# Second layer of the first mixture turned round: weights stationary, shares multiplied into h, output kept by columns

## The chip, the cores and the metric

The kernel runs on one core of a Trainium2 chip. Its time is the device time of one execution in microseconds (us); lower is better. Engines are named as in the profile: PE is TensorE (matmuls; PEld its weight loads), DVE VectorE, ACT ScalarE, POOL GpSimd, SP the queue that issues nearly all DMAs.

## What is computed

Three stages, all in float32. First an attention with random features (4 batches, 8 heads, 576 tokens, head width 64) gives `x`, 2304 tokens by 512. Then two mixtures of experts:

```python
# first mixture: 4 experts, every token through every expert, weighted by its share p
p = domain_probs / (domain_probs.sum(-1, keepdims=True) + 1e-09)
out = np.zeros((N, D), dtype=np.float32)          # N = 2304, D = 512, F = 1024
for e in range(E):
    h = np.maximum(x @ w1[e], 0.0)
    out += p[:, e:e + 1] * (h @ w2[e])
...
# second mixture: 32 slots, 8 experts of 4 slots each; x is now the output of the first
logits = x @ phi
d = softmax of logits over the tokens             # axis 0
slot_input = d.T @ x
for e in range(E):
    h = np.maximum(slot_input[e] @ w1[e], 0.0)
    slot_out[e] = h @ w2[e]
c = softmax of logits over the slots              # axis 1
out = c @ slot_out
```

## The kernel before

Nearly all of the time is the first mixture. Its two layers are cut into 24 **units**: 8 groups of weights (4 experts, each hidden width of 1024 in two groups of 512; `G`) times 3 blocks of 768 tokens (`b`), block innermost. In a unit each layer is one 2x2 block product done with seven products instead of eight (Winograd's form of Strassen's rule; I1 to I7, issued as I1, I2, I6, I5, I7, I3, I4). The first three units compute their first layer plainly, with eight products (`plain1`). Every float32 operand is split into a rounded part (`...h`) and the rest (`...l`), both in the fp32r format, and a product is the sum of three matmul passes, high-high, high-low and low-high.

A first-layer product (`pass1`, line 586) holds 128x128 of w1 stationary and streams 384 token columns of x: 12 matmuls. It leaves h transposed, hidden width on the partitions, tokens along the columns. A second-layer product (`product2`, line 793) holds 128 tokens of h stationary and streams 256 columns of w2: 3 token tiles x 2 x 3 passes = 18 matmuls. Its result has tokens on the partitions, so that the token's share `pr` is one number per partition, and `to_x2` (line 775) adds `pr` times the result to the output tile `x2`, three instructions of 256 columns for each quarter of the output.

PE's order is written out by hand in `pieces`: the first-layer product of unit u and the second-layer product of unit u-1 take turns. What DVE and ACT do between them (sums of the seven products, relu, splitting h into high and low parts) is queued by `evacuate1` and `rest` with a delay in products (`after(d, ...)`, counted down by `tick`). The first-layer results use two PSUM accumulators, X and B, of two banks each and one buffer each; the second layer has two more, so that all eight banks are in use. An accumulator is written again only when all its readers are done. The splitting of the input blocks into the operands of the seven products (`whole`, `block_sum`, `block_split`) runs on DVE and ACT in units 0 to 4, at places given by a table (`prep_steps`).

The second mixture needs, before its experts, a running softmax over the tokens: the **slot work**. For a block of tokens it turns x2 (`slot_turn`, tile tpm), forms logits (`slot_logits`, lq; `slot_sum`, lt), takes the running maximum on DVE and the exponentials on ACT, turns them back (`slot_back`, dp) and gathers `d.T @ x` (`slot_gather`, acc). In the kernel before there are five such blocks (512 tokens, the last 256). So that it can start early, the last two units run their second layer in two parts, two token tiles and then one (`SPLIT`, `LO`, `HI_`; tiles Xq, Bq), with two PSUM banks instead of four, and slot tasks are popped from a list between products.

Behind that comes a tail: 32 tiles of 1 MB of the second mixture's weights (`w2t`), three of them loaded early (`pre`), the others as the memory of the first mixture comes free, in the order of a list (`order`); `hidden` (line 1241), `second_layer` (line 1269) and the output (`out_pair`, line 1295).

## Time and profile before

| | |
|---|---|
| Time, median of 3 runs | 970.72 us (969.58 to 973.63) |
| Profiled execution | 970.0 us, of which 968.2 us lie between the first and the last instruction (the span) |
| PE busy | 944.9 us, 98% of the span |
| DVE, ACT, POOL busy | 699.6, 502.1, 348.2 us (72%, 52%, 36%) |
| DMA | 227.18 MB, 235 GB/s over the span |
| Granted TensorE clock | 0.998 of full speed |

Busy times come from instruction records of that one execution. Matmuls overlap in the pipeline: a record of one lasts 0.28 to 0.34 us, while the next starts 0.12 to 0.17 us later, so a busy PE is not PE at its best, and the time of a product is read from one start to the next. The waits of an engine are put down to what ended them.

### The profile page before, as it was taken

To read this page: it belongs to the slowest core of one execution; us is meant where nothing else is said; L and a number is where in the kernel's file an instruction comes from. 1 tells how busy PE (TensorE), PEld (TensorE's weight loads), DVE (VectorE), ACT (ScalarE), POOL (GpSimd) and SP (SyncE) were. 2 spreads that over 40 slices of the span, in tenths; PEclk is the share of its full clock that TensorE was granted. 3 is DMA by queue.
4 is the path that set the end of the run, shared out by engine and by line. 5 is a ranking of instruction groups with operands and counts; after the bars stand their busy time and mean duration, and the time that the engine had idled before them with its cause. 6 is when DMAs were issued, how large, how long until landed. Compare 5 with 4: busy or idle time off the path is not lost.

```text
span 968.2 us, 18074 instructions
## 1 busy us (share of the span) xinstructions
PE 944.9 (98%) x7070; PEld 902.8 (93%) x7070; DVE 699.6 (72%) x1268; ACT 502.1 (52%) x940; POOL 348.2 (36%) x288
## 2 busy tenths in 40 slices
PE   8999999999999999999999999999999999998997
PEld 8999989999999999999999999999999999796644
DVE  7888885998788766678667687666786667757432
ACT  5899885544554443555444545435454444435322
POOL 7878882343414340443234143404432341000000
PEclk9999999999999999999999999999999999999999
DMA  8688776756787757676666566565656564438997
GB/s 283 187 253 285 246 227 242 224 189 234 268 275 258 232 183 252 226 262 221 234 196 220 188 236 224 185 231 196 224 184 235 193 218 158 133 126 342 380 419 316
DMA packets 63220, 227.18 MB, mean 235 GB/s; under 512 B 8352, under 2 KB 17696, under 8 KB 59040
## 3 DMA queue, kind: packets, MB, share of 16 engines
q1 hardware_dynamic: 59392, 215.81, 65.3%
q10 hardware_dynamic: 3744, 10.23, 2.7%
q8 instruction: 56, 0.92, 0.4%
q14 instruction: 28, 0.23, 0.1%
HBM read 202.42 MB, written 23.59 MB: 233 GB/s over the span
## 4 chain that ended last, share of the span: by engine, by line
PE 88%; DVE 7%; ACT 3%; issue 1%; DMA 1%; SPq 0%; ACTq 0%; DVEq 0%
PE X L586 20%; PE X L793 18%; PE B L586 15%; PE B L793 13%; PE kv L220 3%; PE num L244 3%; PE Xq L793 2%; PE pj L176 2%; PE so L1269 2%; PE Bq L793 1%; PE pj L177 1%; PE pj L178 1%; PE hq L1241 1%; PE tp L234 1%; PE tpx L265 1%
## 5 line engine op out<-in xcount | busy, mean ns | idle before, releaser
L417 POOL TENSOR_TENSOR Tw<-raww 128x512 f32<-128x512 f32 x30 | 43.3, 1465 | 200.1 <-DMA raww<-wl 200.1
L586 PE MATMUL B<-x,w1h 128*128 128x384 f32 x432 | 110.3, 336 | 0.7 <-PE X L793 0.7
L586 PE MATMUL X<-x,w1h 128*128 128x384 f32 x432 | 110.4, 336 | 0.1
L586 PE MATMUL X<-x,w1x 128*128 128x384 f32 x504 | 94.8, 336 | 0.1
L653 DVE TENSOR_TENSOR u<-B,u 128x768 f32<-128x768 f32 x23 | 22.0, 957 | 99.5 <-PE B L586 99.5
L201 ACT ACTIVATE fe<-pj,nb 128x128 f32<-128x128 f32 x288 | 83.2, 390 | 10.0 <-DVE nb L194 9.2
L586 PEld LDWEIGHTS X<-x,w1x 128*128 128x128 f32 x504 | 86.0, 188 | 2.2 <-issue 1.9
L586 PEld LDWEIGHTS B<-x,w1h 128*128 128x128 f32 x432 | 75.4, 189 | 0.9 <-PE X L793 0.9
L586 PEld LDWEIGHTS X<-x,w1h 128*128 128x128 f32 x432 | 75.5, 189 | 0.2 <-PE Xq L793 0.2
L586 PE MATMUL X<-x,w1l 128*128 128x384 f32 x216 | 72.3, 335 | 0.0
L586 PE MATMUL B<-x,w1l 128*128 128x384 f32 x216 | 72.3, 335 | 0.0
L436 POOL TENSOR_TENSOR w2l<-Tw,w2h 128x512 fp32r<-128x512 f32 x32 | 43.3, 1354 | 43.3 <-ACT w2h L435 43.3
L436 POOL TENSOR_TENSOR w2l<-raww,w2h 128x512 fp32r<-128x512 f32 x24 | 31.8, 1325 | 74.6 <-ACT w2h L435 74.5
L184 DVE TENSOR_REDUCE stat<-pj 128x4 f32<-128x512 f32 x72 | 49.5, 687 | 10.0 <-PE pj L178 9.1
L151 POOL TENSOR_TENSOR lo<-raw,hi 128x512 fp32r<-128x512 f32 x35 | 44.8, 1279 | 20.0 <-ACT hi L148 19.4
L436 POOL TENSOR_TENSOR w1l<-raww,w1h 128x512 fp32r<-128x512 f32 x25 | 38.7, 1550 | 34.5 <-ACT w1h L435 34.5
L635 ACT CAST s3h<-X 128x768 fp32r<-128x768 f32 x21 | 16.9, 804 | 65.8 <-DVE X L573 61.9
L436 POOL TENSOR_TENSOR w1x<-Tw,w1x 128x512 fp32r<-128x512 f32 x21 | 29.1, 1386 | 52.4 <-ACT w1x L435 52.4
L586 PE MATMUL B<-x,w1x 128*128 128x384 f32 x252 | 47.4, 336 | 0.0
L176 PE MATMUL pj<-om_hi,hi 128*128 128x256 f32 x144 | 45.1, 313 | 1.6 <-ACT fe L201 1.1
L775 DVE SCALAR_TENSOR_TENSOR x<-B,pr,x 128x256 f32<-128x256 f32 x108 | 45.6, 478 | 1.3
L840 ACT COPY v<-X 128x768 f32<-128x768 f32 x42 | 33.7, 802 | 18.1 <-PE X L793 17.6
(306 smaller groups left out, 3209.5 us busy)
## 6 DMA issues: line engine op xcount, KB each, us to landing
x<-xt SPq DMA_DIRECT2D x84, 768.0 KB, 4.4
x<-xd SPq DMA_DIRECT2D x75, 768.0 KB, 4.5
raww<-wl SPq DMA_DIRECT2D x16, 1024.0 KB, 7.6
w2tb<-w2l SPq DMA_DIRECT2D x11, 1024.0 KB, 10.3
raw<-ql SPq DMA_DIRECT2D x18, 512.0 KB, 4.4
xd<-xst SPq DMA_DIRECT2D x36, 256.0 KB, 2.8
raw<-kl SPq DMA_DIRECT2D x16, 512.0 KB, 4.6
w2ta<-w2l SPq DMA_DIRECT2D x5, 1024.0 KB, 9.4
```

The source lines that it names most:

```text
L151: (nc.gpsimd if i else nc.vector).tensor_tensor(out=lo, in0=r, in1=f32(hi), op=ALU.subtract)
L176: nc.tensor.matmul(o, lhsT=hi[:, pi, :], rhs=om_hi, start=True, stop=False)
L184: nc.vector.tensor_reduce(out=stats(i)[:, 4 * g:4 * g + 4, 0], in_=pjs[i, g], axis=AX.X, op=ALU.max)
L201: nc.scalar.activation(out=feats[i][:, 4 * g + h, :], in_=pjs[i, g][:, h, :], func=AF.Exp, bias=biases[i, g][:, h:h + 1], scale=1.0,)
L220: nc.tensor.matmul(kvps[b][h // 4][:, h % 4, :], lhsT=feats[i][p0:p0 + np_, h, :], rhs=v[p0:p0 + np_, h, :], start=first and h % 4 == 0, s ...
L244: nc.tensor.matmul(num[p0:p0 + n, h, :], lhsT=fts[i][:, 4 * g + h, p0:p0 + n], rhs=kvt[b][:, 4 * g + h, :], start=True, stop=True,)
L417: nc.gpsimd.tensor_tensor(out=out_, in0=a, in1=b_, op=op)
L436: nc.gpsimd.tensor_tensor(out=lo, in0=src, in1=f32(hi), op=ALU.subtract)
L586: nc.tensor.matmul(o, lhsT=lhs[:, jp, c], rhs=rhs[:, :, k, :], start=first and not k and not n, stop=False, skip_group_check=True,)
L775: nc.vector.scalar_tensor_tensor(out=o, in0=src, scalar=w, in1=o, op0=ALU.mult, op1=ALU.add)
L793: nc.tensor.matmul(q[:, n, :], lhsT=lhs[:, jp, p, :], rhs=rhs[:, jp, :], start=i in (I1, I2, I7) and n % 2 == 0 and jp == 0 and m == 0, st ...
L840: nc.scalar.copy(out=v("v1"), in_=q)
```

## The change

- **Second layer turned.** `product2` now holds 128x128 of w2 stationary and streams 384 token columns of h: 2 column tiles x 2 x 3 passes = 12 matmuls. The result has output columns on the partitions; `x2` is kept so ([P, 4, 768] for each token block).
- **Shares into h.** A share now varies along the columns. The shares are turned once, kept in DRAM (`prd`), and for each unit one DMA spreads 768 of them over all partitions (`load_share`, tile prb). `scaled` replaces the relu: max(q, 0) times the share, on DVE, once for each of the four quarters of h. Since h carries the share, the second-layer result is added to `x2` with one instruction for each of the seven products (`evacuate2`); in the first group ACT copies four of them instead.
- **No split ending.** The last two units run like the others. All slot work stands behind the last first-layer product, between the seven second-layer products of the last unit (`ENDING`), in six blocks of 384 tokens. Logits are formed straight from x2; x2 is still turned for the gather.
- **Around it.** The table of `prep_steps` has other places, memory is laid out anew, five weight tiles instead of three are loaded early, and the shares of the second mixture (`slot_shares`) are computed at once behind the slot work. Token halves are now tiles 0-2 and 3-5.

```diff
-        for n, p in enumerate(ps):
-            for jp in range(2):
-                for m, (lhs, rhs) in enumerate(((h, wh), (h, wl_), (l, wh))):
-                    nc.tensor.matmul(
-                        q[:, n, :], lhsT=lhs[:, jp, p, :], rhs=rhs[:, jp, :],
+        for c in range(2):
+            cs = slice(c * P, (c + 1) * P)
+            for jp in range(2):
+                for m, (lhs, rhs) in enumerate(((wh, h), (wl_, h), (wh, l))):
+                    nc.tensor.matmul(
+                        q[:, c, :], lhsT=lhs[:, jp, cs], rhs=rhs[:, jp, :],
...
+    def evacuate2(u, i, q):
+        G, b = units[u]
+        half, n = {I1: (0, 0), I2: (0, 0), I6: (1, 0), I4: (1, 0), I5: (1, 1), I7: (1, 1), I3: (0, 1)}[i]
+        o = x2[b][:, 2 * n:2 * n + 2, half * TH:(half + 1) * TH]
+        if G or i in (I2, I4, I7):
+            nc.vector.tensor_tensor(out=o, in0=q, in1=o, op=ALU.add)
         else:
-            nc.vector.scalar_tensor_tensor(out=o, in0=src, scalar=w, in1=o, op0=ALU.mult, op1=ALU.add)
+            nc.scalar.copy(out=o, in_=q)
...
+    def load_share(u):
...
+        nc.sync.dma_start(
+            out=t.rearrange("p a (n t) -> p (a n) t", n=NP),
+            in_=prd[TB * b:TB * b + TB, GROUPS[G][0], :].partition_broadcast(P),
+        )
+
+    def scaled(u, out, in0, half):
+        w = prb[u][:, half, :].unsqueeze(1).to_broadcast([P, 2, TH])
+        nc.vector.scalar_tensor_tensor(out=out, in0=in0, scalar=0.0, in1=w, op0=ALU.max, op1=ALU.mult)
...
         elif i == I7:
...
+            r = pair(tmp("r22"))
+            if not plain:
+                tt(r, q, pair(L["u4"]), ALU.add)
+            scaled(u, r, q if plain else r, 1)
+            done.add(("r22", u))
         elif i == I3:
...
-            plus(s1, q, pair(L["u4"]), ALU.add)
-            plus(q, q, r11, ALU.subtract)
...
+            scaled(u, o, q, 1)
+            q = o
+            tt(s1, q, pair(L["r22"]), ALU.add)
+            tt(q, q, r11, ALU.subtract)
+            after(0, ("s2", u), lambda: tt(s2, s1, r11, ALU.subtract))
...
-    SPLIT = "q1 P1 q2 q6 P2 q5 P6 q7 q3 P5 q4 r1 P7 r2 r6 P3 r5 P4 r7 r3 r4"
-    ENDING = "q1 t t q2 t q6 t q5 t q7 t q3 t q4 t t r1 r2 r6 t r5 r7 t r3 t r4"
...
+    ENDING = (
+        "l0 P1 l1 t0 P2 t1 l2 b0 P6 a0 t2 l3 b1 P5 a1 t3 g0 P3 b2 a2 l4 g1 P7 b3 a3 t4 g2 P4 b4 a4 g3"
+    )
...
-            (2, 8): [(W, 2, KH[2])],
-            (2, 10): [(W, 2, KH[3])],
+            (2, 9): [(W, 2, KH[2])],
+            (2, 10): [(S, 1, I7)],
```

In `ENDING`, P1 to P4 are the products of the last unit and l, t, a, b, g the five slot steps (logits, sum, turns, back, gather) with the number of the token block.

How the order of instructions changes, at three places (PE's and DVE's rows without their numbers; "x2" at a row's end is a count).

PE, in the middle of the program: the end of one first-layer product into B and the beginning of the second-layer product that follows it; before, the triple of L793 stands six times.

```order
L586 MATMUL B_5629<-x,w1h 128x384 x2
L586 MATMUL B_5629<-x,w1l 128x384
L793 MATMUL B_5652<-w2h,e12h 128x256
L793 MATMUL B_5652<-w2l,e12h 128x256
L793 MATMUL B_5652<-w2h,e12l 128x256
```

Of the change, the same place in the last units (the triple of L771 stands four times):

```order
L597 MATMUL B_9079<-x,w1h 128x384 x2
L597 MATMUL B_9079<-x,w1l 128x384
L771 MATMUL B_9095<-e22h,w2h 128x384
L771 MATMUL B_9095<-e22h,w2l 128x384
L771 MATMUL B_9095<-e22l,w2h 128x384
```

The second layer's rows are as wide as the first layer's now, and there are 12 of them where there were 18.

DVE in unit 21 (token block 2, so that x_2 is written by unit 20's second layer), from first-layer product I7 to I4. Before:

```order
L653 TENSOR_TENSOR u_9539<-B_9571,u_9539 128x768
L836 TENSOR_TENSOR v_9565<-B_9592,v_9565 128x768
L775 SCALAR_TENSOR_TENSOR x_2_3673<-v_9565,pr,x_2_3673 128x256 x3
L573 SCALAR_TENSOR_TENSOR s_9627<-X_9397,u_9539 128x768
L573 SCALAR_TENSOR_TENSOR X_9397<-X_9397,u_9410 128x2x384
L699 TENSOR_TENSOR s_9628<-s_9627,u_9410 128x768
L639 TENSOR_TENSOR s3l<-X_9397,s3h 128x768
L775 SCALAR_TENSOR_TENSOR x_2_3673<-X_9418,pr,x_2_3673 128x256 x3
L653 TENSOR_TENSOR B_9571<-B_9571,u_9499 128x2x384
L573 SCALAR_TENSOR_TENSOR e12l<-B_9571,e12h 128x768
L573 SCALAR_TENSOR_TENSOR u_9499<-B_9571,s_9628 128x768
```

Of the change:

```order
L654 TENSOR_TENSOR r_8576<-B_8563,u_8534 128x768
L584 SCALAR_TENSOR_TENSOR r_8576<-r_8576,prb 128x768
L793 TENSOR_TENSOR x_2_3573<-B_8585,x_2_3573 128x2x384
L584 SCALAR_TENSOR_TENSOR X_8413<-X_8413,prb 128x2x384
L654 TENSOR_TENSOR s_8611<-X_8413,r_8576 128x768
L654 TENSOR_TENSOR X_8413<-X_8413,u_8426 128x2x384
L654 TENSOR_TENSOR s_8612<-s_8611,u_8426 128x768
L648 TENSOR_TENSOR s3l<-X_8413,s3h 128x768
L793 TENSOR_TENSOR x_2_3573<-X_8432,x_2_3573 128x2x384
L654 TENSOR_TENSOR B_8563<-B_8563,u_8497 128x2x384
L584 SCALAR_TENSOR_TENSOR s_8659<-B_8563,prb 128x768
L648 TENSOR_TENSOR e12l<-s_8659,e12h 128x768
```

Three multiplications by the share (L584) have come in here, one of them ahead of the four instructions that read the accumulator X, and each group of one addition and three L775 has become one addition (L793).

PE at the end of the slot work, just ahead of the first `hidden` matmul. Before, from the last turns behind the last product of the last unit on:

```order
L1013 MATMUL tpm<-ident,x_2_3673 128x128 x6
L1074 MATMUL dp<-ident,mo 128x64 x4
L1013 MATMUL tpm<-ident,x_2_3673 128x128 x2
L1092 MATMUL acc<-x_2_3673,d 32x512 x4
L1022 MATMUL lq<-x2t,phis 32x256 x4
L78 MATMUL warm<-om_hi 128x256 x2
L1033 MATMUL lt<-mo,sumr 128x256
L78 MATMUL warm<-om_hi 128x256 x7
L1074 MATMUL dp<-ident,mo 128x32 x2
L1174 MATMUL tps<-sf,mo 128x32 x4
L1182 MATMUL acc<-x_2_3673,d 32x512 x2
L1174 MATMUL tps<-sumr,mo 128x32 x4
```

Of the change, from the last product on:

```order
L996 MATMUL dp<-ident,mo 128x64 x3
L932 MATMUL tpm<-ident,x_2_3573 128x128 x12
L1014 MATMUL acc<-sp_u_9334,keep 32x512
L1014 MATMUL acc<-sp_s_9341,keep 32x512
L1014 MATMUL acc<-sp_s_9348,keep 32x512
L945 MATMUL lq<-x_2_3573,phis 32x384 x4
L932 MATMUL tpm<-ident,x_2_3573 128x128 x8
L955 MATMUL lt<-mo,sumr 128x384
L1014 MATMUL acc<-mo,keep 32x512 x2
L1014 MATMUL acc<-sp_u_9292,keep 32x512
L932 MATMUL tpm<-ident,x_2_3573 128x128 x4
L996 MATMUL dp<-ident,sp_u_9245 128x32 x3
```

The chain of the last block is the same in kind; the turns of the last two blocks, which stood partly ahead of the last products, and one gather more stand behind them now.

## Rows read from the trace of the kernel before

**Rows 1.** The page: engines, and one DMA issue (count, KB each, us to landing).

```profile
PE 944.9 (98%) x7070; PEld 902.8 (93%) x7070; DVE 699.6 (72%) x1268; ACT 502.1 (52%) x940; POOL 348.2 (36%) x288
...
x<-xt SPq DMA_DIRECT2D x84, 768.0 KB, 4.4
```

**Rows 2.** Busy time by stretch: PE, PEld, DVE, ACT, POOL, granted clock, DMA share, GB/s.

```profile
480.00:520.00 40.00, 40.00 (x286) 40.00 (x286) 31.93 (x43) 20.92 (x30) 16.12 (x12) 1.00 0.65 215
```

**Rows 3.** The chain that ended last: start, us until the next piece, engine, line.

```profile
174.89 2.08 PE X L586 x12
...
760.83 2.08 PE B L586 x12
762.91 2.15 PE B L793 x18
...
918.05 7.07 PE hq L1241 x64
```

**Rows 4.** The same chain, slot work on PE near the end.

```profile
861.23 0.87 PE tpm L1013 x8
...
886.51 1.07 PE lq L1022 x8
...
889.21 0.86 PE lt L1033 x2
...
895.31 1.07 PE acc L1092 x8
...
914.09 1.08 PE tps L1174 x8
```

**Rows 5.** The same chain, one slot sum on DVE and ACT.

```profile
873.25 0.61 DVE mt L1041
874.08 0.79 ACT mo L1045 x2
874.89 0.59 ACT mo L1048
```

**Rows 6.** PE in order of time, two waits of the slot work, the last product.

```profile
875.52 0.46 PE L1074 MATMUL dp<-ident,mo 64*128 64x64 f32 x4 [1.42 <-ACT mo L1048]
...
907.26 0.28 PE L793 MATMUL Bq<-w2h,e22l 128*128 128x256 f32 x1
```

**Rows 7.** DVE in order of time, instructions of units in mid program.

```profile
503.40 0.96 DVE L639 TENSOR_TENSOR s3l<-X,s3h 128x768 fp32r<-128x768 f32 x1
...
530.67 0.94 DVE L573 SCALAR_TENSOR_TENSOR s<-X,u 128x768 f32<-128x768 f32 x1
531.54 0.95 DVE L573 SCALAR_TENSOR_TENSOR X<-X,u 128x768 f32<-128x768 f32 x1
...
540.03 1.27 DVE L775 SCALAR_TENSOR_TENSOR x<-B,pr,x 128x256 f32<-128x256 f32 x3
...
571.34 2.05 DVE L639 TENSOR_TENSOR s1l<-s,s1h 128x768 fp32r<-128x768 f32 x1
```

**Rows 8.** PE in order of time, the next unit's first product into X.

```profile
506.66 0.52 PE L586 MATMUL X<-x,w1h 128*128 128x384 f32 x2
```

**Rows 9.** Waits of the whole run: us in total, times, longest.

```profile
DVE u L653 <- PE B L586: 99.5, 22, 6.2
...
DVE v L836 <- PE B L793: 22.5, 19, 1.2
```

**Rows 10.** DMA issues by SP in order of time, and the last weight tile's landing.

```profile
870.48 4.46 SPq L1228 DMA_DIRECT2D w2ta<-w2l  x5
...
901.82 7.55 SPq L1228 DMA_DIRECT2D w2tb<-w2l  x9
...
933.02 0.33 SPq L1228 DMA_DIRECT2D w2t__10926<-w2l  x1
...
w2t__10926<-w2l SPq DMA_DIRECT2D x1, 1024.0 KB, 19.8
```

**Rows 11.** PE in order of time, the matmuls that read that tile.

```profile
955.53 1.05 PE L1269 MATMUL so<-w2t__10926,ht 128*32 128x256 f32 x16
```

More of the change, by code (lines that the diff above doesn't have):

```diff
@@ L693, in evacuate1 @@
+            r = pair(L["u1"])
+            o = r if plain else q
+            scaled(u, o, q, 0)
+            high(0, I1, o)
+            if not plain:
+                after(3, ("r11", u), lambda: nc.scalar.copy(out=r, in_=q))
+            low(0, I1, o)
+        elif i == I7:
+            r = pair(tmp("r22"))
+            if not plain:
+                tt(r, q, pair(L["u4"]), ALU.add)
+            scaled(u, r, q if plain else r, 1)
+            done.add(("r22", u))
         elif i == I3:
             s1, s2, r11 = pair(tmp("s1")), pair(tmp("s2")), pair(L["u1"])
-            plus(s1, q, pair(L["u4"]), ALU.add)
@@ L883, in body @@
     pieces = []
-    for u in range(NU - 2):
+    for u in range(NU):
         for i in range(8 if u < XB else 7):
+            if u + 1 < NU and i == 0:
+                pieces.append(lambda u=u: load_share(u + 1))
             pieces.append((plain if u < XB else up)(u, i))
@@ L989, in body @@
+    keep = lgs = None
     tot = mp.tile([P, 1], F32, name="tot")
     mrun = [mp.tile([P, 1], F32, name=f"mrun{i}") for i in range(2)]
-    def slot_tasks(b):
-        turns = [lambda i=i: slot_turn(b, i) for i in range(4)]
-        logits, total, back, gather = (lambda f=f: f(b) for f in (slot_logits, slot_sum, slot_back, slot_gather))
-        share1, share2 = (lambda f=f: f(b) for f in (slot_share1, slot_share2))
-        if b < NB - 3:
-            wait = [[]] if b == 0 else []
-            tasks = [turns[0:2], turns[2:], [], [logits], [total], [], [back], *wait, [gather], [share1], [share2]]
-        elif b == NB - 3:
-            tasks = [turns[0:2], turns[2:], [logits], [total], [], [back], [gather]]
-        else:
-            tasks = [turns[0:2], turns[2:], [logits], [total]]
-        return [lambda fs=fs: [f() for f in fs] for fs in tasks]
@@ L1007, in slot_turn, with slot_task @@
-    def slot_turn(b, i, k0=0, k1=NK):
-        if i == 0 and k0 == 0:
-            st["x2t", b] = stg.tile([P, NK, 4, P], F32, name="x2t", tag="raw")
-        tp = bank("s", "tpm").rearrange("p (k t) -> p k t", k=NK)
-        for k in range(k0, k1):
-            nc.tensor.transpose(tp[:, k, :], x2t(SB[b][0] + i)[:, k * P:(k + 1) * P], ident)
-        nc.scalar.copy(out=st["x2t", b][:, k0:k1, i, :], in_=tp[:, k0:k1, :])
+    def slot_task(s):
+        {"l": slot_logits, "t": slot_sum, "a": slot_turns, "b": slot_back, "g": slot_gather}[s[0]](int(s[1]))
@@ new lines, in body, with spare_place, slot_turn @@
+    places = {}
+    def spare_place(n):
+        if n not in places:
+            if n < 6:
+                t = w1e.tile([P, 6, DM], F32, name="mo", tag="w1x")
+                places.update({k: t[:, k] for k in range(6)})
+            else:
+                tag = ("u1", "u2", "s1", "s2", "u4", "r22")[n - 6]
+                places[n] = lt.tile([P, DM], F32, name=f"sp_{tag}", tag=tag)
+        return places[n]
+    mo = spare_place
+    def slot_turn(n, i):
+        b, c0 = n // 2, (n % 2) * TH + i * P
+        x = spare_place(4 + (n % 2) * 3 + i)
+        tp = bank("s", "tpm").rearrange("p (k t) -> p k t", k=NK)
+        for k in range(NK):
+            nc.tensor.transpose(tp[:, k, :], x2[b][:, k, c0:c0 + P], ident)
+        copy = nc.vector.tensor_copy if n == NB - 1 and i == 1 else nc.scalar.copy
+        copy(out=x, in_=tp.rearrange("p k t -> p (k t)"))
+        st["x2t", n, i] = x
@@ L1153, in body @@
     assert not later, [n for _, _, n, _ in later]
-    while side:
-        task()
+    pp["2"].release()
+    pp["T"] = bank_pool("psT", "left", (4, 5, 6, 7))
+    groups.update({"aq": [4], "bq": [5], "a": [2, 3, 0], "b": [1, 4], "c": [5, 6], "d": [7]})
     n = NB - 1
+    s2 = mo(11)
+    nc.gpsimd.memset(s2[NS * NP:P], 0.0)
+    slot_logits(n)
     slot_turn(n, 0)
-    slot_turn(n, 1, 2, 4)
-    slot_back(n - 1)
-    slot_turn(n, 1, 0, 2)
-    acc = slot_gather1(n - 1)
-    slot_logits(n)
-    slot_gather2(n - 1, acc)
-    keep_warm(2, "qx")
+    slot_turn(n, 1)
     slot_sum(n)
-    keep_warm(7, "qx")
+    slot_gather(n - 1)
+    slot_turn(n, 2)
     sf = mp.tile([P, NS], F32, name="sf")
@@ L1179, in body @@
     slots_turn(0, mo(0), sf)
-    acc = bank("aq", "acc")[0:64, :]
-    for i in range(2):
-        nc.tensor.matmul(
-            acc[32 * i:32 * i + 32, :], lhsT=st["d", n][:, i, :], rhs=x2t(NT - 2 + i), start=True, stop=True
-        )
-    s2 = mo(1)[0:64, :]
-    nc.scalar.copy(out=s2[:, 0:HD], in_=acc[:, 0:HD])
-    nc.vector.tensor_copy(out=s2[:, HD:DM], in_=acc[:, HD:DM])
-    slots_turn(1, s2, sumr[0:64, 0, :])
+    acc = slot_gather1(n)
+    nc.scalar.copy(out=s2[0:NS * NP, 0:HD], in_=acc[:, 0:HD])
+    nc.vector.tensor_copy(out=s2[0:NS * NP, HD:DM], in_=acc[:, HD:DM])
+    slots_turn(1, s2, sumr[:, 0, :])
     st["rest"]()
@@ L1352, in body @@
     wqa.release()
-    gap.release()
     prep.release()
+    stg.release()
     const.release()
```

461 lines of the change are left out of this document (179 added, 282 removed).

## The prediction

> **What bounds the kernel now.** The page first: PE is busy 98% of the span, DVE 72% [rows 1]. The stretches of 40 us come next: in the middle of the program PE is busy all the time at full clock, and DVE 31.9 of 40 us [rows 2]. So there PE alone sets the pace, and what the other engines do matters only where they make PE wait. The chain of waits says the same and gives the prices: from 174.89, where unit 1 begins, it is a train of products, 2.08 us for 12 matmuls of 384 columns and 2.15 us for 18 of 256 [rows 3]. The train, with the slot work in it, ends at 918.05, where `hidden` begins [rows 3].
>
> Between 174.89 and 918.05 lie 743.2 us. They hold 163 first-layer products (two units of 8, 21 of 7, and not unit 0's 8) and 168 second-layer products: 163 x 2.08 + 168 x 2.15 = 700.2 us. The split into two and one token tiles in the last units leaves the number of matmuls as it is. Slot work on PE, at the chain's prices [rows 4]: 72 turns in runs of 8 at 0.87 make 7.8 us, four and a half logits at 1.07 make 4.8, as many sums at 0.86 make 3.9, as many gathers at 1.07 some 5.0, two tps at 1.08 make 2.2, and turning back with the warm-up matmuls some 3.1: 26.8 us. What is left, 743.2 - 700.2 - 26.8 = 16.2 us, are waits of PE. All but about 2 us of them fall into the last two units and the slot work: the 629.5 us from 174.89 to the first product of unit 22 hold 149 and 147 products and a part of one more, 627.4 us.
>
> Behind 918.05 come 50.2 us of tail. In it PE runs without a gap worth naming to the last weights: they are asked for at 933.02, land 19.8 us later at 952.8 [rows 10], and PE reads them at 955.53 [rows 11]. So the tail is PE's work in a row with the weights' stream 3 us ahead of it.
>
> **The change part by part, from the profiled execution's 970.0 us.**
>
> *Wide second-layer products.* 168 times, 18 matmuls of 256 columns become 12 of 384: the same 4608 columns, fewer starts. The first layer's rows are this very form, at 2.08 against 2.15 us [rows 3]. Gain 0.07 x 168 = 11.8 us. The bounds: nothing, if a matmul with h streaming is no faster for its columns than now; 11.8, the whole difference.
>
> Per matmul the rows give 119 ns for 256 columns and 173 ns for 384, so a fixed part near 13 ns each at 2.4 GHz, which is the level that the granted clock of 1.00 means [rows 2, 3]. The Trainium skill, "TensorE: Matmul & The Clock Gate", section "Back-to-back issue gap", gives a fixed part of 2.5 ns for a lone stream; by that six matmuls fewer would save 15 ns a product and 2.5 us in all, and the sum below would come out 9.3 us higher. The rows are of this kernel's own pairs of weight load and matmul, so I go by them; the other is a rival below.
>
> *DVE's work.* In the first layer four multiplications by the share take the place of relus on ACT and of sums with a relu in them: four instructions more in each unit, each like the ones of 768 columns from PSUM that follow each other by 0.87 us [rows 7], so +3.5 us. In the second layer three additions of about 0.96 and four groups of three at 1.27 [rows 7], 8.0 us, become seven additions, 6.7 us. That is +2.2 us a unit. DVE now stands idle 99.5/22 = 4.5 us a unit ahead of one addition and 22.5/19 = 1.2 us ahead of another [rows 9], of some 29.6 us. So it stays under PE, with 3 us or more to spare. In the first group, where ACT copies four results, DVE has less to do than now. The early units also carry the splitting of the inputs, at new places; unit 3 has 27 of DVE's instructions in 29.2 us, and I allow 1.5 us of PE's waiting there.
>
> Where the new instruction can hurt is accumulator X. Its last reader, s3l, ends at 504.36 (503.40 + 0.96), and the next unit's first product wants X at 506.66 [rows 7, 8]: 2.3 us of slack. The multiplication ahead of the four readers takes 0.87 of it. 1.4 us are left, so PE doesn't wait. All else that PE waits for (operands split with delays of up to ten products) has more than a product of slack.
>
> Of DVE's instructions, those with both inputs in SBUF vary: 0.95 us as a rule, 2.05 at 571.34 [rows 7]. The Trainium skill, "SBUF — State Buffer", section "Who interferes with whom", says that a VectorE instruction with two SBUF inputs locks against a GpSimd one that reads SBUF. That speaks against the change: it has eight such instructions a unit where there were five. At the observed extreme of 1.1 us each they would cost DVE 3.3 us more in a unit, about its spare time.
>
> *The share's DMA.* 24 times 0.39 MB, half of an operand load of 768 KB, which lands in 4.4 us [rows 1]. It is asked for a unit (29 us) ahead. The DMA engines are 65% busy [rows 2]; at the 215 GB/s there it is 1.8 us of traffic a unit. It waits on SP for DVE's last use of the same buffer, about 2 us after the last product of a unit; behind it stand operand loads that have three products (12 us) of lead. I cost it at nothing; if the lead were gone it would be the 4.4 us of a load each time.
>
> *The ending.* Slot work on PE is as much as now: 72 turns, logits and sums over the same 2304 columns, six gathers of about 1.05 instead of four and a half, without the warm-up, 27 us. What changes is the waiting. Now the last two units run with two PSUM banks for the second layer and DVE's short instructions, and 14 of the 16.2 us of waits are there. After the change they run like the others, and the slot work has the last unit's seven products to hide in. A block's sum takes 0.61 on DVE and 0.79 and 0.59 on ACT [rows 5], 2.1 us with the handovers, and PE meets it with a wait of 1.42 [rows 6]. In the new order there are 2 to 4 us of other PE work between each sum and its `slot_back`: a product and more for blocks 1 to 4, one product, a sum and a logits for block 0. ACT's copies of the turns (0.6 us each, three banks ahead) will cost a wait here and there; I take 2 us for them. Then the last block, whose chain runs now from 907.4 (the last product's last matmul starts at 907.26 [rows 6], one start lasts 0.12) to 918.05, 10.7 us, of which about 2.5 are waits. It will be the same chain with one gather and four turns more on PE, so 11 to 12 us with the same waits. So waits after the change: 2 in the train as now, 1.5 in unit 3, 4.5 in the ending, 8 in all, instead of 16.2. Gain 8.2 us; bounds: nothing, if the ending waits as now, and 12 us, if only the train's 2 and the last chain's 2.5 remain.
>
> *The tail* is the same PE work behind `hidden`'s start, so 50.2 us. Its cover is the weights' stream: 27 tiles are left instead of 29. The first of them can go when the operand loads end (some 10 us ahead of the last first-layer product, about 840), three more with that product, the rest as products, turns and gathers release memory, one behind the other on SP. Nine tiles in a row, issued 7.55 us long from 901.82 [rows 10], and the ten behind them, land by 952.8: 19 in 47 us at most, 2.45 us each. If the stream starts in earnest only with the turns of the second token block, some 12 us ahead of `hidden`, the 20 tiles that are then left take 49 us and end 37 us after `hidden` begins; PE wants the last one at 37.5 (955.53 - 918.05). So it just holds even then. The doubt is worth 1 or 2 us.
>
> The sum: 970.0 - 11.8 - 8.2 = 950.0 us. `hidden` would begin near 898, the span be 948. The profiled execution is 0.7 below the median of the runs, so 950.7; I forecast 951.
>
> **The rivals.**
>
> *The ending waits as it did.* Six blocks' chains in one product each, every turn copied by ACT, DVE with its backlog from the last unit: the 14 us of waits stay. For it: PE's order is strict, so that one late copy holds all products behind it. Against it: the room counted above. 951 + 8 = 959 us.
>
> *Wide matmuls don't pay,* that is, the change doesn't do what it says: by the fixed part of 2.5 ns the product takes 2.13 us. Against it the rows of the first layer, of the same width. 960 us.
>
> *DVE becomes the bound,* the one on the other side. It has one place: X's release. If DVE reaches I3's sums with a backlog or the instructions with two SBUF inputs stretch, s3l ends later than the 1.4 us of slack, and PE waits in each unit. The gain of 20 us is used up when X comes 2.4 us later than worked out in each of 20 units (1.4 of slack, 1.0 of wait). Half as much again (3 us late) gives 982. For it: three more instructions that lock, and only some 3 us of idle time. Against it: DVE is waiting for PE at I7, just ahead of that place, 4.5 us long now.
>
> *The weights come late.* If a tile of the first sixteen waits for a release behind it in SP's order, `hidden` waits: 10 us would give 961.
>
> **How the numbers follow.** The forecast (945 to 956) has 0.62; the ending as now 0.14; wide matmuls that don't pay 0.06; late weights 0.08; DVE the bound 0.10. Half of the last is a mild wait that eats part of the gain (955 to 966), half ends at no change or slower. The range reaches from 944, the ending without its waits and a tail that is 2 us shorter, to 964, which takes in the rivals at 959 to 961: 0.85. What a measurement of this kernel can tell from no change is about 0.5%, 5 us. Faster by more than that: all cases but the second half of DVE's and a part of its first, 0.92; the same 0.04; slower 0.04.
>
> **What would show it.** Right: second-layer products at 2.08 us in the chain, unit after unit 29.1 to 29.2 us; PE without waits on DVE between 180 and 850; the first lq near 853; `hidden` between 895 and 903, 50 us ahead of the end; DVE busy about 80%. Wrong: PE waiting for s3l at each unit's first product (DVE); L771's matmuls 177 ns apart (width); PE waiting for ACT's copies of tpm, or dp for ACT, by 10 us or more in the last 45 us ahead of `hidden` (ending); PE waiting on a DMA of w2t (weights).

## The result and the profile after

The changed kernel takes 958.15 us (median of 4 runs, 956.87 to 961.01), the kernel before 971.57 us on the same chip (969.58 to 973.63): ratio 0.9866, 95% interval 0.9832 to 0.99. It is 13.4 us faster where 20 were forecast. The time lies in the range of 944 to 964, but 2 us above the 945 to 956 that had most of the chance. The profiled execution took 959.41 us, its span 957.6.

From the page, what answers to [rows 1]: DVE is busier, 79% where it was 72%, as forecast, and an operand load lands in 5.2 us in place of 4.4, with the new share loads (prb) beside it.

```profile
PE 936.4 (98%) x6065; PEld 892.4 (93%) x6065; DVE 752.8 (79%) x1134; ACT 428.8 (45%) x841; POOL 354.5 (37%) x290
...
x<-xt SPq DMA_DIRECT2D x84, 768.0 KB, 5.2
...
prb<-prd SPq DMA_DIRECT2D x23, 384.0 KB, 6.2
```

The chain that ended last, in mid program and at the tail's beginning [rows 3]. Both layers' products take 2.08 us now. The tail's first 64 matmuls take 8.63 us where they took 7.07.

```profile
780.01 2.08 PE B L771 x12
782.09 2.08 PE X L597 x12
...
905.85 8.63 PE hq L1149 x64
```

PE in order of time: the first second-layer product, a wait with the matmul behind it, a product behind another wait, and the first logits of the slot work.

```profile
178.89 0.33 PE L771 MATMUL X<-e11h,w2h 128*128 128x384 f32 x1
...
226.07 0.44 PE L771 MATMUL X<-s1l,w2h 128*128 128x384 f32 x1 [2.65 <-DVE s1l L648]
...
259.40 3.31 PE L597 MATMUL X<-x,w1x 128*128 128x384 f32 x12 [2.68 <-ACT u L668]
...
861.06 0.85 PE L945 MATMUL lq<-x,phis 128*32 128x384 f32 x8
```

From 178.89 to 861.06 lie 682.2 us and 323 products (162 of the first layer, 161 of the second). At 2.08 us they need 671.8, so PE loses 10.3 us there; this difference is called **the loss** below and is formed in the same way for every run. The forecast had 3.5 us for it. Busy time by stretch (PE, PEld, DVE, ACT, POOL, granted clock, DMA share, GB/s) shows where it lies: at mid program, as in [rows 2], PE is never idle; around 225 and 257 it is, and DVE is at 25.9 and 28.0 of 30 us.

```profile
480.00:520.00 40.00, 40.00 (x232) 40.00 (x231) 32.95 (x36) 15.41 (x23) 16.80 (x13) 1.00 0.66 221
...
200.00:230.00 30.00, 27.35 (x150) 27.03 (x148) 25.92 (x26) 9.51 (x13) 10.45 (x6) 0.94 0.62 217
230.00:260.00 30.00, 27.32 (x157) 27.00 (x157) 27.98 (x26) 14.77 (x22) 14.36 (x9) 1.00 0.88 303
...
905.00:910.00 5.00, 4.97 (x32) 1.69 (x35) 3.22 (x9) 0.95 (x2) 0.00 (x0) 0.66 1.02 423
```

What DVE did just ahead of the two stops. Near 224 it makes a sum of the input splitting (L505), then the operand s1l for which PE waits. Near 256 it makes such a sum, then s4 (L723).

```profile
221.41 0.95 DVE L793 TENSOR_TENSOR x<-B,x 128x768 f32<-128x768 f32 x1
222.28 1.80 DVE L505 TENSOR_TENSOR xr<-xr 128x768 f32<-128x768 f32 x1
224.00 2.01 DVE L648 TENSOR_TENSOR s1l<-s,s1h 128x768 fp32r<-128x768 f32 x1
...
254.21 1.61 DVE L505 TENSOR_TENSOR xr<-xr 128x768 f32<-128x768 f32 x1
255.74 2.04 DVE L723 TENSOR_TENSOR s<-s,s 128x768 f32<-128x768 f32 x1
257.70 0.94 DVE L648 TENSOR_TENSOR e11l<-B,e11h 128x768 fp32r<-128x768 f32 x1
258.57 0.94 DVE L793 TENSOR_TENSOR x<-B,x 128x768 f32<-128x768 f32 x1
259.44 1.65 DVE L648 TENSOR_TENSOR s1l<-s,s1h 128x768 fp32r<-128x768 f32 x1
```

ACT at that second stop: its row is strict, s4h waits for s4, and the copy that PE waits for (u, out of accumulator X) stands behind s4h.

```profile
257.81 0.83 ACT L644 CAST s4h<-s 128x768 fp32r<-128x768 f32 x1 [2.62 <-DVE s L723]
258.55 0.79 ACT L668 COPY u<-X 128x768 f32<-128x768 f32 x1
```

GpSimd at both places: low halves of the next group's weights, then sums of them.

```profile
221.97 1.30 POOL L437 TENSOR_TENSOR w1x<-Tw,w1x 128x512 fp32r<-128x512 f32 x1 [8.34 <-ACT w1x L436]
223.91 1.29 POOL L437 TENSOR_TENSOR w1x<-Tw,w1x 128x512 fp32r<-128x512 f32 x1 [0.65 <-ACT w1x L436]
...
253.71 3.25 POOL L418 TENSOR_TENSOR Tw<-raww 128x512 f32<-128x512 f32 x2 [5.43 <-DMA raww<-wl]
256.92 3.35 POOL L418 TENSOR_TENSOR Tw<-raww,Tw 128x512 f32<-128x512 f32 x2
```

The reader is to see two things in these rows. The DVE operations that take 1.6 to 2.0 us in place of 0.95 lie beside GpSimd's, and have all inputs in SBUF; those that read an accumulator in PSUM (B) take 0.94 beside the same GpSimd work. And each of these two stops costs more than its length. From start to start, the twelve matmuls behind the first take 3.75 us in place of 2.08; the product at 259.40 takes 3.11 and the next 2.75. At the slowest the matmuls are 0.32 us apart in place of 0.173. The granted clock is 0.66 from 225 to 230 and from 260 to 265, the mean of a stretch partly at 1.2 and partly at 2.4 GHz; just before, it is 1.00 (2.4 GHz).

The rest of the missing gain is small and elsewhere: unit 1's first product begins at 176.69 (174.89 before, [rows 3]), and behind 905.85 come 51.75 us of tail, not 50.2.

### The profile page after: what moved, and what is told of

It reads as the page before. It is cut to its first block, busy times and chain, and to the rows that moved or that the text cites. A ratio compares the mean times of both kernels' runs of the same rounds, so it can differ in the third digit from the quotient of the medians.

```text
span 957.6 us, 15793 instructions
## 1 busy us (share of the span) xinstructions
PE 936.4 (98%) x6065; PEld 892.4 (93%) x6065; DVE 752.8 (79%) x1134; ACT 428.8 (45%) x841; POOL 354.5 (37%) x290
## 4 chain that ended last, share of the span: by engine, by line
PE 86%; DVE 8%; ACT 2%; DMA 2%; issue 1%; SPq 0%; ACTq 0%; DVEq 0%
PE X L597 19%; PE X L771 19%; PE B L597 14%; PE B L771 14%; PE kv L221 3%; PE num L245 3%; PE pj L177 2%; PE hq L1149 2%; PE so L1177 2%; PE pj L178 1%; PE pj L179 1%; PE tp L235 1%; PE tpm L932 1%; PE tpx L266 1%; DMA prb<-prd 1%
## 5 line engine op out<-in xcount | busy, mean ns | idle before, releaser
L793 DVE TENSOR_TENSOR x<-X,x 128x768 f32<-128x768 f32 x84 | 80.0, 952 | 40.2 <-PE X L771 39.7
L597 PEld LDWEIGHTS X<-x,w1x 128*128 128x128 f32 x504 | 88.6, 189 | 3.0 <-ACT u L668 3.0
L202 ACT ACTIVATE fe<-pj,nb 128x128 f32<-128x128 f32 x288 | 82.9, 390 | 10.3 <-DVE nb L195 9.6
L597 PEld LDWEIGHTS X<-x,w1h 128*128 128x128 f32 x432 | 78.0, 188 | 1.1 <-PE B L771 0.9
L597 PEld LDWEIGHTS B<-x,w1h 128*128 128x128 f32 x432 | 77.8, 188 | 0.0
L793 DVE TENSOR_TENSOR x<-B,x 128x768 f32<-128x768 f32 x72 | 68.3, 949 | 3.3 <-PE B L771 2.8
L437 POOL TENSOR_TENSOR w2l<-raww,w2h 128x512 fp32r<-128x512 f32 x24 | 36.5, 1532 | 84.0 <-ACT w2h L436 84.0
L668 ACT COPY u<-X 128x768 f32<-128x768 f32 x63 | 50.1, 795 | 24.3 <-PE X L597 24.3
L437 POOL TENSOR_TENSOR w2l<-Tw,w2h 128x512 fp32r<-128x512 f32 x32 | 47.5, 1493 | 31.6 <-ACT w2h L436 31.6
L185 DVE TENSOR_REDUCE stat<-pj 128x4 f32<-128x512 f32 x72 | 49.5, 688 | 11.9 <-PE pj L179 11.1
L644 ACT CAST e11h<-B 128x768 fp32r<-128x768 f32 x21 | 16.9, 803 | 77.3 <-PE B L771 68.7
L644 ACT CAST e12h<-s 128x768 fp32r<-128x768 f32 x24 | 20.1, 836 | 66.9 <-DVE s L584 66.9
```

The lines of the kernel that those rows point to most:

```text
L185: nc.vector.tensor_reduce(out=stats(i)[:, 4 * g:4 * g + 4, 0], in_=pjs[i, g], axis=AX.X, op=ALU.max)
L202: nc.scalar.activation(out=feats[i][:, 4 * g + h, :], in_=pjs[i, g][:, h, :], func=AF.Exp, bias=biases[i, g][:, h:h + 1], scale=1.0,)
L437: nc.gpsimd.tensor_tensor(out=lo, in0=src, in1=f32(hi), op=ALU.subtract)
L597: nc.tensor.matmul(o, lhsT=lhs[:, jp, c], rhs=rhs[:, :, k, :], start=first and not k and not n, stop=False, skip_group_check=True,)
L644: nc.scalar.copy(out=pair(hs[i][0]), in_=src)
L668: nc.scalar.copy(out=pair(tmp({I1: "u1", I6: "u2", I5: "u4"}[i])), in_=q)
```

## The experiments

The question was what makes DVE late in units 1 to 3: the places of the splitting steps in its row (theory A, with E for the passage into unit 3), its sum of work (B), GpSimd beside it (C), or the new DMAs (D). In the table stand the loss and what it is formed from, and two sums over the rows that DVE's timeline shows for 176 to 270 us (a row that only reaches into this stretch counts whole): **excess**, what the instructions longer than 1.1 us take beyond 0.95 each, and **idle**, the idle time that stands at the rows. For the kernel before these two are 6.3 and 10.8 us.

| kernel | median us | first L771 | first lq | loss | excess | idle |
|---|---|---|---|---|---|---|
| changed kernel | 958.15 | 178.89 | 861.06 | 10.3 | 10.9 | 10.1 |
| t1_places_before | 958.54 | 179.52 | 860.70 | 9.3 | 11.8 | 10.4 |
| t2_sums_later | 961.18 | 178.28 | 862.00 | 11.9 | 12.7 | 7.9 |
| t3_pool_apart | 958.81 | 178.39 | 860.43 | 10.2 | 10.1 | 10.3 |
| t5_four_slots | 959.60 | 178.62 | 859.12 | 8.7 | 11.9 | 7.0 |
| t10_unit_2 | 960.02 | 180.05 | 862.01 | 10.1 | 12.4 | 9.1 |
| t11_all | 954.79 | 175.51 | 858.12 | 10.8 | 13.4 | 6.0 |
| t9_no_sums | 956.30 | 178.82 | 856.10 | 5.4 | 11.6 | 11.2 |
| t13_relu_act | 954.37 | 180.29 | 857.45 | 5.3 | 14.0 | 12.9 |
| t12_idle_pool | 948.27 | 178.29 | 851.62 | 1.5 | 0.0 | 11.8 |

Single runs of one kernel differ by 4 us and more, so small effects are read from the loss, not from the medians. But the loss comes from one profiled execution each, and it varies too: t4_warm, whose edit stands behind the first lq, has 11.2 us where the changed kernel has 10.3. So differences of about 1 us in it say nothing. A wait that ends by "issue" below is one for which the profile shows no releaser.

**Places, three ways.** First the table of the kernel before:

```diff
-            (1, 7): [(S, 0, I6)],
-            (1, 8): [(S, 0, I5)],
+            (1, 0): [(S, 0, I6)],
+            (1, 1): [(S, 0, I5)],
...
```

> The table of the splitting steps is that of the kernel before; all else is the changed kernel. Theory A (the two stops of TensorE, 2.65 us near 223 and 2.68 near 257, come from splitting steps that stand in VectorE's row ahead of what the next product needs; the half clock behind each adds about 1.5): both stops go, some 8 us, 950 us, if the old places do not put steps ahead of others. Rival B (VectorE has too much to do in units 1 to 3 wherever the steps stand, for each unit's work grew by 2.2 us): stops of the same sum at other places, 955 to 961.

958.54 us (957.48 to 959.33): no change. The two stops are gone and others have come. The longest of PE's waits from 170 to 290 (us in total, times, longest):

```profile
PE X L772 <- DVE s2l L649: 2.1, 1, 2.1
PE X L598 <- DMA x<-xt: 1.5, 1, 1.5
PE X L772 <- ACT x L796: 0.8, 1, 0.8
```

Then the two sums that stood ahead of the late operands, and the rest of block 2's steps with the second:

```diff
-            (2, 3): [(T, 1, 1)],
-            (2, 5): [(T, 1, 2)],
+            (2, 5): [(T, 1, 1), (T, 1, 2)],
...
-            (3, 2): [(T, 2, 0)],
-            (3, 4): [(T, 2, 1)],
+            (3, 4): [(T, 2, 0)],
+            (3, 5): [(T, 2, 1)],
...
```

> Only the two sums that stood ahead of the late operands move: the second sum of block 1 one place behind the low half s1l, and the first sum of block 2 behind s4, the rest of block 2's steps with it. Theory A: s1l would begin at 222.3 in place of 224.0 and s4 at 254.2 in place of 255.7; what stays is their own slow 2.0 us beside GpSimd, so stops of 1 us or less each, no half clock, a gain of 5 to 8 us: 950 to 953. Theory C (GpSimd's work beside them is the cause, which place the sums have matters little): stops of 2 us or more stay, 956 to 958.

961.18 us (959.85 to 961.86). The waits for s1l and u fall to 0.6 and 0.8 us, and 2.6 of "issue", 1.5 for x<-xt and 1.0 for DVE come instead. Theory A falls with these two: with the steps at other places the loss is as large, in other waits.

Then GpSimd's work at the two places put off:

```diff
-            n = (None, None, I5, I7, I6, I3, I1, I2)[i]
+            for n in ((), (), (), (), (I5, I7), (I6,), (I3, I1), (I2, I4))[i]:
...
-                after(1, ("w2a", G), lambda: ...
+                d = 4 if G == 0 else 0
+                after(1 + d, ("w2a", G), lambda: ...
```

> The sums stay; instead GpSimd's weight splits of unit 2 go two to three products later and its sums of the second layer's weights (first group only) four ticks later, so that GpSimd is idle near 222 to 226 and 253 to 260. Theory C: the VectorE operations that took 1.6 to 2.0 us there take 0.95, s1l ends 1.9 us earlier and s4 1.7 earlier: stops of 0.8 and 1.0 us in place of 2.65 and 2.68, with less of the half clock: 951 to 954. Theory A alone (only the order matters): under 2 us gained, 956 to 958.

958.81 us (956.07 to 960.12). The wait for s1l falls to 0.8 us, that for the copy u goes, and PE now waits for x<-xt (2.4), for GpSimd's own late w1l (2.1) and for ACT's w1h (0.9). At the two places DVE's operations take 0.95 us each:

```profile
222.14 0.95 DVE L505 TENSOR_TENSOR xr<-xr 128x768 f32<-128x768 f32 x1
223.01 0.95 DVE L648 TENSOR_TENSOR s1l<-s,s1h 128x768 fp32r<-128x768 f32 x1
...
252.61 0.95 DVE L505 TENSOR_TENSOR xr<-xr 128x768 f32<-128x768 f32 x1
253.48 0.95 DVE L723 TENSOR_TENSOR s<-s,s 128x768 f32<-128x768 f32 x1
```

At the first, GpSimd is idle up to 232.80; at the second, its sums begin at 253.55, hardly later or sooner than before (253.71), but DVE is there sooner. So both stops shrink as theory C expected, and the run speaks for C. It gains nothing, since w1l and w1h are late through the edit itself, x comes late, and the excess is nearly as large as before: GpSimd's work, moved, meets other DVE operations.

**Two chains of waits shortened.** ACT's wait for the stores of block 0, by two more places for the high halves:

```diff
-        if "xh" not in stage:
-            stage["xh"] = prep.tile([P, 4, 512], F32R, name="xh", tag="pre2")
+        k = "xh0" if b == 0 and nsplit[0] > 2 else "xh"
+        if k not in stage:
+            stage[k] = prep.tile([P, 4, 512], F32R, name="xh", tag="pre0" if k == "xh0" else "pre2")
```

> The high halves of block 0's splits get four places in place of two, so ScalarE need not wait for the stores (6.3 us near 204, behind which VectorE sat idle 3.4 us). Theory B (VectorE has too little time left in units 1 to 3, wherever the steps stand; so each idle or slowed microsecond of it comes back as a stop of TensorE): the idle 3.4 us go, the steps behind come that much earlier, the stop near 223 (2.65 us and about 1.5 of half clock) goes, 954. If instead the order alone counts (theory A): s1l is queued behind the same sum, but all of it earlier, so nearly the same; the two part at the stop near 257, which stays by A and shrinks by B. If the stores were only a symptom of full queues: no gain, 958.

959.60 us (956.36 to 960.66). DVE's idle time falls by 3.1 us and the stop near 223 is gone; the one near 257 stays (2.9 us). The loss falls by 1.6 us only.

And the delays of unit 2's last steps:

```diff
-        ... else (1, 3, 5, 7, 4, 5, 9, 6) if u < XB else ...
+        ... else (1, 3, 5, 7, 4, 5, 9, 6) if u < XB - 1 else (1, 3, 5, 7, 6, 7, 9, 8) if u < XB else ...
```

> Only unit 2's last steps move: the difference s4 two ticks later, its high half two, its low half two, so that in ScalarE's row the copies of the first accumulators of unit 3 stand ahead of s4h, which waits for VectorE. Theory E (the stop near 257 is the passage from the plain units to the first unit with seven products: TensorE waits for a copy on ScalarE that stands behind s4h): that stop and the half clock behind it go, some 4 us before the ending, 954; the stop near 223 stays. Theory B (VectorE has too little time in these units wherever things stand): the lateness comes out at the next operand, 957 to 959.

960.02 us (957.17 to 960.78). The wait for s1l stays, 2.75 us long, and this time the matmuls behind it run at full pace, at a granted clock of 1.00:

```profile
227.97 0.44 PE L771 MATMUL X<-s1l,w2h 128*128 128x384 f32 x1 [2.75 <-DVE s1l L648]
...
229.81 0.51 PE L597 MATMUL X<-x,w1h 128*128 128x384 f32 x2
```

That for u falls from 2.7 to 0.7, and 1.6 for another ACT copy and 1.8 of "issue" come in its place. Theory E falls as theory A did.

All of it together, with two edits outside these units, the bank of the shares' turning and the warm matmuls:

```diff
-            tp = bank("d", "prt")
+            tp = bank("b", "prt")
...
+    keep_warm(2, "d")
     slots_turn(0, mo(0), sf)
...
+    keep_warm(5, "d")
     slots_turn(1, s2, sumr[:, 0, :])
```

> Together: four places for block 0's high halves, unit 2's last steps later, block 2's first sum one place on, the shares' turning in another PSUM bank, and the seven warm matmuls of the ending. Theory E with A: both stops and their half clock go (8.4 us), the wait of 1.5 us near 48 goes, the tail runs at the full clock (1.5 us): 947 to 950. Theory B: the stops come back elsewhere, only the 3 us of the last two are gained: 954 to 956.

954.79 us (954.38 to 955.04), 0.9838 of before (0.9823 to 0.9852). Of the kernels that leave nothing out this is the fastest: all its runs lie below all of the changed kernel's, though the two intervals of the ratio to before overlap. But the loss is 10.8 us, as large as ever, spread over more places:

```profile
PE X L598 <- issue: 2.3, 1, 2.3
PE X L598 <- ACT e22h L645: 1.9, 1, 1.9
PE X L598 <- ACT u L669: 0.8, 1, 0.8
PE B L772 <- DVE x L794: 0.4, 1, 0.4
```

In the profile the gain is that of the two edits outside: the first second-layer product begins at 175.51 in place of 178.89, and the tail, with hq at full clock, is 1.5 us shorter. The turning of the shares had waited 1.46 us in PE's row, since its bank was the one whose result DVE was still reading ("PE prt L852 <- DVE x L257"); with the banks in other turns, a wait of 1.6 us of tpx for ACT's ft went too, which nobody had aimed at.

**The share's DMAs.**

```diff
+        if u > 2:
+            prb[u] = prb[1 + (u - 1) % 2]
+            return
```

> The shares are loaded for the first three units only; later units multiply with an earlier unit's shares (that part of the result is left out). Theory D (the 24 loads of 0.39 MB, 23 of them spread over 128 partitions, crowd the queue: x comes late, stores land late): without 21 of them 2 to 5 us less, 953 to 956. By my forecast, which costed them at nothing: 958, and x<-xt lands in 4.4 us again in place of 5.2.

961.56 us (959.63 to 961.72), no gain. An operand load lands in 4.3 us, as before the change, and both stops are there (2.7 and 2.5 us, loss 10.4). Theory D falls; the price of nothing holds. (The chain of the changed kernel puts s4's start down to the landing of such a load, 6.92 us; here, without that load, s4 begins at 256.01 in place of 255.74.)

**Less work for DVE, two ways.**

```diff
-        nc.vector.tensor_tensor(out=out_, in0=a, in1=b_, op=ALU.subtract)
+        if b == 0: nc.vector.tensor_tensor(out=out_, in0=a, in1=b_, op=ALU.subtract)
```

> The eight sums that VectorE makes for blocks 1 and 2 (1.0 to 1.8 us each, in units 1 to 3) are left out, so the operands of those blocks are the plain blocks and not their differences; nothing else moves. Theory B: with some 11 us less to do between 205 and 270 VectorE is never late, no stop of TensorE over 0.5 us between 187 and 280, 949 to 951. Theory D (transfers are what is late): the stops move to x and to the stores, 955 to 958.

956.30 us (954.36 to 959.95); the loss is halved, 5.4 us. A stop of 1.9 us stays: PE waits for an ACT copy that stands behind s4h, and s4 takes 1.92 us beside GpSimd.

```diff
+        if u < XB:
+            return nc.scalar.activation(out=out, in_=in0, func=AF.Relu)
```

> In units 0 to 2 the shares are left out and ScalarE does the ReLU, as it does much of it in the kernel before: four operations of 0.95 us a unit go from VectorE to ScalarE (0.8 us each), which is what the share costs VectorE there. Theory B (VectorE's sum of work in units 1 to 3, its own and what GpSimd adds, is over what TensorE now leaves it; the share's multiplication is the part that the change added): 11 us less for VectorE, TensorE loses 3 to 5 us where it loses 10.3, 951 to 953. If ScalarE, which waits for VectorE in its row, becomes the late one: 956 to 960.

954.37 us (952.1 to 957.26), loss 5.3 us. Of waits for DVE 0.3 us is left; one of 2.0 us for x<-xt has come, and the twelve matmuls behind it take 3.69 us. So theory B is right that less DVE work helps. But some 11 us less of it bring 5, while the excess stays at 11.6 and 14.0 us.

**GpSimd without work.**

```diff
-        nc.gpsimd.tensor_tensor(out=out_, in0=a, in1=b_, op=op)
+        if G != 1:
+            nc.gpsimd.tensor_tensor(out=out_, in0=a, in1=b_, op=op)
...
-        nc.gpsimd.tensor_tensor(out=lo, in0=src, in1=f32(hi), op=ALU.subtract)
+        if G == 1:
+            lo = hi
+        else:
+            nc.gpsimd.tensor_tensor(out=lo, in0=src, in1=f32(hi), op=ALU.subtract)
```

> GpSimd's sums and low halves for the second group's weights are left out (first-layer and second-layer; the high halves stand in for the low ones, and raw blocks for the sums), so GpSimd has nothing to do beside units 1 to 3; VectorE's and ScalarE's instructions are all there. Theory C2 (VectorE has time enough for its own work, but its operations beside GpSimd take up to 2.0 us in place of 0.95, 10.9 us in all from 176 to 270, and these come out as TensorE's stops): the excess falls under 2 us, TensorE loses 2 to 4 us between the first product of the second layer and the first slot logits where it loses 10.3, 950 to 952. Theory E2 (the chains of ScalarE's copies behind VectorE's differences set the stops, GpSimd little): 956 to 958.

948.27 us (947.8 to 955.73, three of the four runs below 948.5), 9.9 less than the changed kernel; ratio to before 0.9791 (0.9745 to 0.9837). The loss is 1.5 us, 8.8 less; another 1.5 us of the profile's difference is the tail, which ran at full clock in this execution and has nothing to do with GpSimd's work. The only wait of PE from 170 to 860 is 0.5 us for x<-xt. Busy time by stretch: GpSimd has nothing to do, and PE is busy.

```profile
200.00:230.00 30.00, 30.00 (x175) 30.00 (x174) 24.71 (x29) 12.36 (x17) 0.00 (x0) 1.00 0.70 248
230.00:260.00 30.00, 29.48 (x171) 29.20 (x170) 25.39 (x29) 18.08 (x27) 0.00 (x0) 1.00 0.89 321
```

DVE in order of time, the four operations of above in the same order, at 0.95 us each:

```profile
220.20 0.95 DVE L511 TENSOR_TENSOR xr<-xr 128x768 f32<-128x768 f32 x1
221.07 0.95 DVE L654 TENSOR_TENSOR s1l<-s,s1h 128x768 fp32r<-128x768 f32 x1
...
247.61 0.95 DVE L511 TENSOR_TENSOR xr<-xr 128x768 f32<-128x768 f32 x1
248.47 0.95 DVE L729 TENSOR_TENSOR s<-s,s 128x768 f32<-128x768 f32 x1
```

DVE's idle time is no smaller than in the changed kernel (11.8 us), and from the first second-layer product through unit 3 DVE's and ACT's rows hold the same instructions in the same order (some of ACT's copies read the raw weights in place of the sums); only the excess is gone. That PE or ACT had waited for GpSimd's own results is not the reason: among the waits of both from 170 to 290 in the changed kernel none is for POOL.

**The tail.**

```diff
+    keep_warm(2, "d")
     slots_turn(0, mo(0), sf)
...
+    keep_warm(5, "d")
     slots_turn(1, s2, sumr[:, 0, :])
```

> Seven matmuls whose result is not used stand again in the ending's last two waits of TensorE (2 ahead of the first turning of the sums, 5 ahead of the second). If the tail's extra 1.5 us (first stretch of hq 8.63 us where it was 7.07, granted clock 0.66 in 905 to 910) is the clock after those waits: hq at full clock from its first matmul, 956.6. If the tail waits for its weights anyway: 958.1 as now, with the wait moved behind hq.

In the profile hq runs at full clock from its start, and the tail is 956.3 - 906.1 = 50.2 us, 1.5 less than in the changed kernel. The chain's row and the stretch:

```profile
906.11 7.07 PE hq L1151 x64
```

```profile
905.00:910.00 5.00, 4.95 (x47) 2.10 (x50) 3.04 (x9) 1.07 (x3) 0.17 (x1) 1.00 1.02 423
```

The median, 958.48 us (958.11 to 959.0), does not show it. Part of the reason is that the dip does not come in every execution: without warm matmuls t1_places_before, with the same 0.87 us of idle PE ahead of hq, and t12_idle_pool have the 7.07 us too, and the eight other profiles without them have a lower clock there. With them it came in neither profile (this run and t11_all), but two profiles are few.

**The width.**

```diff
-                    nc.tensor.matmul(
-                        q[:, c, :], lhsT=lhs[:, jp, cs], rhs=rhs[:, jp, :],
+                    for t in (slice(0, 256), slice(256, TH)):
+                        nc.tensor.matmul(
+                            q[:, c, t], lhsT=lhs[:, jp, cs], rhs=rhs[:, jp, t],
```

> Each second-layer matmul of 384 columns is cut into one of 256 and one of 128: 12 more matmuls a product, the same columns, nothing else. If each start costs the 13 ns that the two kernels' products give (2.15 us of 18 by 256, 2.08 of 12 by 384): 2.24 us a product, 168 x 0.155 = 26 us more, 984. If a start costs 2.5 ns: 2.11 us and 5 us more, 963. If matmuls of 128 columns run slower for each column, more than 984.

(Both halves carry the flag that begins a sum, so part of each sum is begun anew; columns and starts are as told.) 1066.84 us (1066.61 to 1067.35): 108.7 us more, 0.65 a product, 54 ns for each matmul more. Each of these brings a weight load of its own (8081 on PEld in place of 6065). PE in order of time, pairs of 256 and 128 columns, 0.22 to 0.23 us apart:

```profile
499.73 0.39 PE L772 MATMUL X<-s2h,w2l 128*128 128x256 f32 x2
499.96 0.39 PE L772 MATMUL X<-s2l,w2h 128*128 128x256 f32 x2
```

Neither price of a start told it. Take the 119 ns that one of 256 columns has with the other operand streaming: then one of 128 takes some 108 ns (173 + 54 - 119), about as much, though 128 columns more cost only 54 from 256 to 384. So the run isolates neither the start nor the weight load, and why the narrow matmul is no shorter stays open. The width term itself rests on the chain's 2.08 us.

## Why the prediction was right, and where it was off

**Wide products: right in size.** 168 products at 2.08 us where they took 2.15, 11.8 us. The rival by which they would not pay falls with the chain's rows. That it is a fixed part of 13 ns at each start is not shown: t7_cut's added matmuls cost 54 ns each.

**The ending: right.** From the first lq to hq 44.8 us (861.06 to 905.85), 45 forecast (853 to 898). All of the gain of the old ending's waits came.

**DVE: right for 20 units, wrong for three.** Steady units run without a wait of PE, at 32.95 of 40 us, and DVE's share is 79%, as worked out; s3l, where the prediction looked for the lateness, was never what PE waited for (the second stop was a wait for X all the same, but for ACT's copy u out of it). The step that failed stands at the end of DVE's part: "unit 3 has 27 of DVE's instructions in 29.2 us, and I allow 1.5 us of PE's waiting there", and ahead of it "in the first group ... DVE has less to do than now". Counted by instructions that was so: 81 from 176 to 270 where the kernel before has 105. By time it was not: DVE is busy 83.1 of the 94 us there, 82.7 before, while PE, with the stops, does the work of fewer products in them; and 10.9 us of DVE's rows is excess, 6.3 before. The loss is 10.3 where 3.5 (2 and 1.5) were forecast: a term mis-sized by 6.8 us. Its parts: two stops of 2.65 and 2.68 us, and about 1.7 of lower clock behind each of them in this execution (3.75 in place of 2.08; 3.11 and 2.75 in place of twice 2.08). Behind the same stop in t10_unit_2 the second part did not come.

The cause is shown by t12_idle_pool: with GpSimd idle the same instructions at the same places lose 1.5 us. DVE's records of 768 columns in the changed kernel from 176 to 860 us show which of them GpSimd slows. Of 365 with an input in PSUM none takes over 0.97 us, though 181 lie beside a GpSimd instruction. Of 139 with all inputs in SBUF and GpSimd idle none takes over 0.96. Of 86 with all inputs in SBUF beside GpSimd 48 take more than 1.1, up to 2.09. The prediction had seen the lock (2.05 us at 571.34 [rows 7]) and had priced it at "3.3 us more in a unit, about its spare time", but for the steady units, and looked for it at s3l, X's last reader on DVE. It bit where the splitting steps, all of them with both inputs in SBUF there, share units 1 to 3 with GpSimd's work on the next weights. The rival "DVE becomes the bound" had the mechanism and the wrong place; its mild half, 955 to 966 us, with a chance of 0.05, is what came. That the time still lies in the range is in part luck: the range was made that wide for the rivals at 959 to 961, and none of them came. The Trainium skill, "SBUF — State Buffer", section "Who interferes with whom", says that a VectorE instruction with two inputs in SBUF contends with a GpSimd one that reads SBUF, and that one with at most one SBUF input, outside its two-port modes, does not. By that rule the trace agrees: 1.61, 2.04 and 1.65 us beside GpSimd with two SBUF inputs, 0.94 and 0.94 between them with one in PSUM.

**The start and the tail: priced at nothing, 1.8 and 1.55 us.** The turning of the shares was not in the sum; it waits 1.46 us for its bank. The tail's 50.2 us were taken as given although the change removes the warm matmuls, whose absence was counted only as less work: hq's first 64 matmuls took 1.56 us more, at a granted clock of 0.66 from 905 to 910, behind 0.87 us of idle PE from 900 to 905. In t1_places_before and t12_idle_pool as much idle PE was followed by no lower clock. The weights did not come late.

The sum: 950.0 + 6.8 + 1.8 + 1.55 - 0.2 (ending) = 960.0 us, and the profiled execution took 959.41.

What stays open is a cure that leaves nothing out, and why the clock falls behind some stops and ahead of the tail in most executions and not in all. Also open is how far one can get: in t1, t2, t3, t13 and t12 a wait for x<-xt (0.5 to 2.4 us) came up near 252 to 259. Neither other places (t1, t2, t3, t10) nor shorter chains (t5, t11) brought the loss below 8.7 us. Doing GpSimd's weight work ahead of unit 1 was not tried.

## What to carry to other kernels

When a change makes PE faster, every stage in which another engine was just in time has to be costed again, stage by stage: here PE needed 0.5 us less in each unit (7 x 0.07), units 4 to 23 had room for it, units 1 to 3 had not. Count DVE's work there by the durations that it has beside GpSimd, not by its number of instructions; a sum over the records of what they take beyond their undisturbed time is quickly formed. And where one stop goes and another of the same size comes, moving steps further is no use: take away a whole engine's work for one run, and the cause names itself.

## What the runs showed of the hardware

- A DVE instruction of 768 columns with an input in PSUM took 0.94 to 0.97 us with and without GpSimd beside it; with all inputs in SBUF it took 0.95 alone and up to 2.09 beside GpSimd (changed kernel, 176 to 860 us).
- A matmul of 128 columns with its weight load took about as long in this stream as one of 256 (an estimate of 108 ns from t7_cut, against 119), so cutting 384 into 256 and 128 cost 54 ns for each cut, four times the fixed part that was worked out from the wider ones.
- Behind stops of PE of 2.6 to 2.9 us the next twelve matmuls mostly took 3.1 to 3.8 us from start to start, and the granted clock of that stretch fell (changed kernel 0.66, t5_four_slots 0.76). But behind one of 2.75 us in t10_unit_2 they took 2.2, at a clock of 1.00. Behind a stop of 2.0 in t13_relu_act they took 3.69, behind one of 2.1 in t3_pool_apart 2.2.
- Where one transposition writes its PSUM bank can move the waits of a whole stage. In t11_all, with the shares' turning in another bank, the first second-layer product began 3.4 us sooner; only 1.5 of that was the wait aimed at. t11_all has other edits beside it, and t5_four_slots, which has one of them alone, began 0.3 us sooner.
